# Loading the second query weight from ScalarE's DMA queue, beside the second K block

## The chip, the cores and the metric

The kernel runs on one NeuronCore of one Trainium2 chip. The metric is the device time of one execution in microseconds (us); lower is better.

## The reference

Two independent attention blocks, A and B, are computed for one new token each (decode), and their outputs are put side by side. Both have 32 heads of width 128 and a cache of 8192 keys and values in bf16; here B also has one K/V head per query head, so both blocks do the same work.

```python
def block(x, k_cache, v_cache, wq, wo):          # x [1,1,512], wq [512,4096], wo [4096,512]
    q = (x @ wq).reshape(1, 1, 32, 128).transpose(0, 2, 1, 3)
    scores = einsum("bhqd,bhkd->bhqk", q, k_cache) * 128 ** -0.5   # caches [1,32,8192,128]
    p = softmax(scores, axis=-1)
    o = einsum("bhqk,bhkd->bhqd", p, v_cache)
    return o.transpose(0, 2, 1, 3).reshape(1, 1, 4096) @ wo
out = concatenate([block(A...), block(B...)], axis=-1)             # [1,1,1024] bf16
```

Each cache element is used once, so the kernel mostly moves data: 4 caches of 67 MB, and 4 weights of 4 MB.

## The kernel before

The 64 heads are taken four at a time, in `NM` = 16 steps (0 to 7 belong to A, 8 to 15 to B). A step `n` loads one K block and one V block of four heads, 8192 KB each: a partition holds 256 rows of one head, in one run of 64 KB. K blocks go to the two slots of `kn`, V blocks to the single buffer `vn`. A query weight `wq` is 4096 KB, 32 KB per partition, and the two of them are put into the two halves of `vn` before the first V block needs that space.

In a step, VectorE (DVE) multiplies K in place by the broadcast query in four chunks (`plan_mul`, L348), TensorE (PE) adds up groups of products by matmuls with an identity (`plan_red`, L357), DVE finishes the sums (`plan_sr`, L368), finds the maxima (`plan_max`, `plan_gmax`, L374 and L383), ScalarE (ACT) takes the exponentials (L405), and one step later PE multiplies them with V (`plan_pv`, L426). All 128 partitions get the query from `plan_q`: for each half of a block's heads a group of 16 matmuls reads `wq` (L326) and ACT copies the result from PSUM to `qbc` (L334).

Every engine's program is an ordered list. `op` appends an instruction behind waits for what it `needs`; `dma` appends a transfer to the list of the engine that issues it. Before the change SyncE (SP) issues all loads, in the order in which the planner meets them:

- A's `wq` and the two rows `x`, K of step 0, B's `wq`;
- K of step 1, which waits for the copies of `x` (`x_ready`), because `x` lies in its slot;
- V of step 0, which waits for `q_done[1]`, the last query matmul of B, because both `wq` lie in `vn`;
- K of step 2, which waits for the last reduction of step 0 (`red_done`), then V of step 1 (waits for `pv_done` of step 0), K of step 3, and so on.

On PE, the two query groups of A come first. Those of B stand in step 0 behind the third reduction and ahead of the fourth. On ACT, the two copies of `x` and the two copies for A come first, then the two copies for B, then step 0's exponentials.

The order around the change, with the planner's calls:

```python
load_k(0)
load_wq(1)
plan_sel()
for j in range(QA // 4):
    plan_q(0, j)
for n in range(NM):
    ...
```

Of the kernel before, what the change touches and what calls it, by code (L numbers as in the profile page):

```python
# [11 lines left out]
P = 128  # L12
# [11 lines left out]
class _Plan:  # L24
# [15 lines left out]
    def op(self, eng, fn, ctr=None, needs=(), inc=1):  # L40

        for m in needs:
            self.wait(eng, m)
        self.prog[eng].append((fn, ctr, inc))
        if ctr is None:
            return None
        ctr.n += inc
        return ctr, ctr.n
# [81 lines left out]
def bass_concat_heads__mha_block_cached__gqa_block_cached__decode_kernel(  # L130
# [16 lines left out]
    wqs = [A_wq, B_wq]  # L147
# [27 lines left out]
    with ExitStack() as st:  # L175
# [8 lines left out]
        def flat(ap):  # L184
            return ap.rearrange("p t d -> p (t d)")
# [3 lines left out]
        wq_buf = [flat(vn[:])[:, a * W:(a + 1) * W] for a in range(NA)]  # L189
# [48 lines left out]
        def ctr(name):  # L238
            return _Ctr(nc, st, name)

        s_x = ctr("s_x")
        s_w = [ctr("s_w%d" % a) for a in range(NA)]
# [7 lines left out]
        def dma(eng, dst, src, c, needs=()):  # L250
            return op(eng, lambda e: e.dma_start(dst, src), c, needs, inc=16)  # L251
# [22 lines left out]
        k_in, v_in, wq_in, wo_in = {}, {}, {}, {}  # L274
# [6 lines left out]
        def load_k(n):  # L281
            k_in[n] = dma("SP", flat(kn[:, n % NK]), quad(ks, n), s_k[n % NK],
                          [x_ready if n == KX else red_done.get((n - NK, NCH - 1))])
# [4 lines left out]
                                [q_done[1] if n == 0 else pv_done[n - 1]]))  # L288
                       for i, (t0, t1) in enumerate(zip(cuts, cuts[1:]))]

        def load_wq(a):
            wq_in[a] = dma("SP", wq_buf[a], wqs[a].rearrange("(p c) n -> p (c n)", p=P), s_w[a])

        def load_wo(a, g):
            h0, n = WOG[a][g]
            src = wos[a][h0 * Dh:(h0 + n) * Dh, :].rearrange("(p j) n -> p (j n)", p=P)
            wo_in[a, g] = dma("SP", wo_sb[a][:, h0:h0 + n, :].rearrange("p j n -> p (j n)"), src,
                              s_wo[a][g], [red_done[NM - 2, NCH - 1]])


        load_wq(0)
        x_in = [dma("SP", xrow[0:1, a, :], xs[a][0], s_x) for a in range(NA)][-1]

# [14 lines left out]
        def plan_q(a, j):  # L318

            def mm(e):  # L320
                r = None
                for hh in range(G):
                    for c in range(C):
                        w = wq_sb[a][:, c, 4 * G * j * Dh:4 * G * (j + 1) * Dh].rearrange(
                            "p (i h d) -> p i h d", h=G, d=Dh)[:, :, hh, :]
                        r = e.matmul(  # L326
                            qyp[hh * HP:(hh + 1) * HP, :].rearrange("p (i d) -> p i d", d=Dh),
                            xb[:, a, c, hh * HP:(hh + 1) * HP], w,
                            start=(c == 0), stop=(c == C - 1))
                return r  # L330
            m = op("PE", mm, c_pe, [x_ready, wq_in[a], qy_free[0]])
            q_done[a] = m
            n0 = a * QA + 4 * j
            qy_free[0] = op("ACT", lambda e: e.copy(  # L334
                qbc[:, n0:n0 + 4, :].rearrange("p i d -> p (i d)"), qyp[:]), c_act, [m])
            for n in range(n0, n0 + 4):
                qbc_ready[n] = qy_free[0]
# [8 lines left out]
        def plan_mul(n, c):  # L346
            k = kn[:, n % NK, c * CT:(c + 1) * CT, :]
            mul_done[n, c] = op("DVE", lambda e: e.tensor_tensor(  # L348
                k, k, qbc[:, nth(n), :].broadcast_to([P, CT, Dh]), ALU.mult),
                c_mul, [k_in[n], qbc_ready[n]])  # L350

        def plan_red(n, c):

            def mm(e, i0):
                r = None
                for i in range(Dh // DW):
                    r = e.matmul(  # L357
                        rps[:, c % 2, :].rearrange("p (t d) -> p t d", d=DW), ident[:],
                        kn[:, i0, c * CT:(c + 1) * CT, i * DW:(i + 1) * DW],
                        start=(i == 0), stop=(i == Dh // DW - 1))  # L360
                return r
            by_slot = (n % NK, [lambda e, i=i: mm(e, i) for i in range(NK)])
            red_done[n, c] = op("PE", by_slot, c_red, [
                i_ident, mul_done[n, c],
                sr_done[n, c - 2] if c > 1 else sr_done.get((n - 1, c + NCH - 2))])

        def plan_sr(n, c):
            sr_done[n, c] = op("DVE", lambda e: e.tensor_reduce(  # L368
                s_sb[:, c * CT:(c + 1) * CT],
                rps[:, c % 2, :].rearrange("p (t d) -> p t d", d=DW), AX.X, ALU.add),  # L370
                c_sr, [red_done[n, c], p_done.get(n - 1)])

        def plan_max(n):
            m_done[n] = op("DVE", lambda e: e.tensor_reduce(  # L374
                m1[:], s_sb[:], AX.X, ALU.max), c_dve, [sr_done[n, NCH - 1]])
# [33 lines left out]
        def plan_sum(n):  # L409
            m = op("PE", lambda e: e.matmul(misc[:, 0:G], ones_f[:], rsum[:],  # L410
                                            start=True, stop=True), c_pe,
                   [p_done[n], misc_free[0]])
            r_done[n] = misc_free[0] = op("DVE", lambda e: e.reciprocal(
                rinv[:, nth(n), :].rearrange("p o g -> p (o g)"), misc[:, 0:G]), c_dve, [m])

        def plan_pv(n, t0, t1):
            for t, landed in v_in[n]:
                if t < t1:
                    wait("PE", landed)
            wait("PE", p_done[n])  # L420
            wait("PE", o_done.get(n - 1))

            def mm(e):
                r = None
                for t in range(t0, t1):
                    r = e.matmul(acc[:, 0:G], vn[:, t, :], pt[:, t, :],  # L426
                                 start=(t == 0), stop=(t == T - 1))
                return r
            if t1 == T:
                pv_done[n] = op("PE", mm, c_pv)  # L430
            else:
                op("PE", mm)

        def plan_o(n):
            o_done[n] = op("DVE", lambda e: e.tensor_tensor(  # L435
                oD[:].rearrange("p a h -> p (a h)")[:, nth(n, G)], acc[:, 0:G],
                rinv[:, nth(n), :].rearrange("p o g -> p (o g)"), ALU.mult),
                c_dve, [pv_done[n], r_done[n]])
# [4 lines left out]
        def plan_sel():  # L443
            sel_ready[0] = op("DVE", lambda e: e.tensor_reduce(
                sel[:, QR - 1:QR], ident[:, 0:P:QR], AX.X, ALU.max), c_dve, [i_sel0, i_ident])
            for g in RG:
                v = ident[:].rearrange("p (s j) -> p s j", j=g)
                op("DVE", lambda e, g=g, v=v: e.tensor_reduce(mask[g][:], v, AX.X, ALU.max),
                   c_dve, [i_ident])
                sel_ready[g] = op("DVE", lambda e, g=g, v=v: e.tensor_reduce(  # L450
                    jsel[g][:], v.rearrange("p s j -> p j s"), AX.X, ALU.max), c_dve)
# [108 lines left out]
        dcuts = []  # L560

        load_k(0)
        load_wq(1)
        plan_sel()
        for j in range(QA // 4):
            plan_q(0, j)
        for n in range(NM):
            if n >= L0:
                cuts[n].append(len(pl.prog["PE"]))
                dcuts.append(len(pl.prog["DVE"]))  # L570
            if n + 1 < NM:
                load_k(n + 1)
            else:
                load_wo(0, 0)
                for g in range(BEFORE):
                    load_wo(1, g)
            plan_mul(n, 0)
            plan_red(n, 0)
            plan_mul(n, 1)
            plan_red(n, 1)  # L580
            plan_sr(n, 0)
            plan_mul(n, 2)
            plan_red(n, 2)
            plan_sr(n, 1)
            plan_mul(n, 3)
            plan_sr(n, 2)
            if n == 0:
                for j in range(QA // 4):
                    plan_q(1, j)
            else:  # L590
                cuts[n].append(len(pl.prog["PE"]))
                plan_sum(n - 1)
                for t0, t1 in zip(VLAST, VLAST[1:]):
                    plan_pv(n - 1, t0, t1)
                cuts[n].append(len(pl.prog["PE"]))
                plan_o(n - 1)
            plan_red(n, 3)
            plan_sr(n, 3)
            plan_max(n)
            plan_gmax(n)  # L600
            plan_exp(n)
            load_v(n, VLAST if n == NM - 1 else (0, T))
# [119 lines left out]
```

## Time and profile before

| | |
|---|---|
| time, median of 3 runs | 666.3 us (666.25 to 666.35) |
| span of the profiled execution | 665.0 us |
| the profiled execution's own time | not given apart from its span; the median is 1.3 us above the span |
| PE busy | 440.2 us (66%) |
| DVE busy | 342.1 us (51%) |
| ACT busy | 62.4 us (9%) |
| bytes moved | 285.32 MB, mean 429 GB/s |

A profile is of one execution. Times in it are from its first instruction. Engine names with a q (SPq, ACTq) are the sequencers that issue transfers; a transfer's time to landing runs from its issue to the semaphore that says that all of it is there. In a timeline a row has the start, the duration, the engine, the line, the operation and how many were merged (x16); in brackets stands how long the engine had been idle and what released it. In the chain of waits a row has start, duration and what was waited for. Rows of queues give packets, MB and the share of the time of 16 DMA engines.

### The profile page before, as it was taken

The page shows a single profiled execution, that of the slowest core. Times are in us where ns is not written, and L with a number is a line of the kernel's source. Part 1 is how long each engine was busy: PE and PEld are TensorE (multiplying, and loading weights), DVE is VectorE, ACT ScalarE, POOL GpSimd, SP SyncE. Part 2 cuts the span into 40 slices and gives each one's busy share as a digit, 9 for nine tenths or more (in the row PEclk, how much of TensorE's full clock was granted, in tenths as well). Part 3 has the DMA queues.
Part 4 walks back from the last instruction along what each step waited for, and adds up shares of the span by engine and source line. Part 5 has one row for each costly group of instructions (what it writes and reads, how often), then busy time and mean ns, then how long its engine had stood idle before and what let it go on. Part 6 is the DMA issues. An engine that isn't in the chain of part 4 may idle for free.

```text
span 665.0 us, 12196 instructions
## 1 busy us (share of the span) xinstructions
PE 440.2 (66%) x5513; PEld 249.2 (37%) x5513; DVE 342.1 (51%) x218; ACT 62.4 (9%) x151; POOL 3.0 (0%) x15
## 2 busy tenths in 40 slices
PE   1166857848488594838759383875948387594875
PEld 0022343616135261614526161452616144262625
DVE  1085907466390746639073663908356380835620
ACT  1002002020200102020010202010020201002020
POOL 1000000000000000000000000000000000000000
PEclk9999857768786676878667687966768796676885
DMA  9999999999999999999999999999999999999997
GB/s 380 436 447 435 439 428 438 414 439 438 426 438 441 434 438 418 438 438 422 441 441 434 438 418 438 434 426 441 441 434 434 418 441 434 426 441 441 404 438 317
DMA packets 6069, 285.32 MB, mean 429 GB/s; under 512 B 683, under 2 KB 942, under 8 KB 1198
## 3 DMA queue, kind: packets, MB, share of 16 engines
q1 hardware_dynamic: 6056, 285.22, 99.3%
q8 instruction: 5, 0.08, 0.0%
q14 instruction: 2, 0.02, 0.0%
q10 hardware_dynamic: 6, 0.00, 0.0%
HBM read 285.21 MB, written 0.00 MB: 429 GB/s over the span
## 4 chain that ended last, share of the span: by engine, by line
DMA 65%; PE 24%; DVE 8%; issue 2%; SPq 0%; ACT 0%; DVEq 0%
DMA kn<-in_B_k_cache_dram 20%; DMA kn<-in_A_k_cache_dram 17%; DMA vn<-in_A_v_cache_dram 14%; PE rps L357 13%; PE acc L426 10%; DMA vn<-in_B_v_cache_dram 9%; DVE kn L348 8%; DMA kn<-in_B_wo_dram 4%; PE qyp L326 0%; SPq L251 0%; DVE s_sb L368 0%; PE yrow L538 0%; ACT qbc L334 0%; PE misc L410 0%; DVEq L348 0%
## 5 line engine op out<-in xcount | busy, mean ns | idle before, releaser
L357 PE MATMUL rps<-kn,ident 128*128 128x512 bf16 x1024 | 290.4, 451 | 168.4 <-DVE kn L348 165.3
L348 DVE TENSOR_TENSOR kn<-kn,qbc 128x8192 bf16<-128x8192 bf16 x64 | 281.5, 4419 | 93.3 <-DMA kn<-in_A_k_cache_dram 53.8
L357 PEld LDWEIGHTS rps<-kn,ident 128*128 128x128 bf16 x1024 | 111.4, 113 | 334.5 <-issue 258.1
L426 PE MATMUL acc<-pt,vn 128*128 128x4 bf16 x4096 | 109.3, 165 | 10.9 <-DMA vn<-in_B_v_cache_dram 5.9
L426 PEld LDWEIGHTS acc<-pt,vn 128*128 128x128 bf16 x4096 | 108.5, 101 | 11.8 <-DMA vn<-in_B_v_cache_dram 6.3
L368 DVE TENSOR_REDUCE s_sb<-rps 128x64 f32<-128x512 f32 x64 | 44.0, 688 | 110.9 <-PE rps L357 110.9
L405 ACT ACTIVATE pt<-s_sb,negb 32x256 bf16<-32x256 f32 x64 | 54.8, 857 | 1.9
L397 ACT ACTIVATE negb<-bmp 128x1 f32<-128x1 f32 x16 | 2.7, 171 | 526.6 <-PE bmp L393 526.6
L435 DVE TENSOR_TENSOR oD<-acc,rinv 128x4 f32 (+1 forms) x16 | 2.6, 162 | 96.3 <-PE acc L426 96.3
L393 PE MATMUL bmp<-gm,hrow 1*128 1x1 f32 x128 | 18.4, 260 | 6.0 <-DVE gm L383 6.0
L393 PEld LDWEIGHTS bmp<-gm,hrow 1*128 1x128 f32 x128 | 17.1, 203 | 10.7 <-DVE gm L383 10.0
L380 PE MATMUL mtp<-ident_f,m 128*1 128x128 f32 x32 | 6.1, 271 | 19.8 <-DVE m L374 19.8
L405 ACT ACTIVATION_READ_ACCUMULATOR pt<-s_sb,negb 32x1 f32 x64 | 15.9, 248 | 0.0
L380 PEld LDWEIGHTS mtp<-ident_f,m 128*1 128x1 f32 x32 | 1.4, 81 | 27.7 <-DVE m L374 27.7
L308 PE MATMUL misc<-ones_bf,kn 1*128 1x128 bf16 x4 | 0.6, 305 | 13.0 <-DMA kn<-in_B_x_dram 13.0
L383 DVE TENSOR_REDUCE gm<-mtp 1x4 f32<-1x128 f32 x16 | 4.5, 279 | 7.5 <-PE mtp L380 7.5
L326 PE MATMUL qyp<-vn,xb 128*32 128x512 bf16 x64 | 6.0, 505 | 2.2 <-ACT qbc L334 1.5
L410 PEld LDWEIGHTS misc<-rsum,ones_f 128*128 128x128 f32 x32 | 6.0, 190 | 2.9 <-issue 0.7
L374 DVE TENSOR_REDUCE m<-s_sb 128x1 f32<-128x256 f32 x16 | 6.7, 420 | 0.5
L334 ACT CAST qbc<-qyp 128x512 bf16<-128x512 f32 x4 | 2.3, 586 | 39.3 <-PE qyp L326 39.3
L308 PEld LDWEIGHTS misc<-ones_bf,kn 1*128 1x128 bf16 x4 | 0.3, 132 | 13.0 <-DMA kn<-in_B_x_dram 13.0
L410 PE MATMUL misc<-rsum,ones_f 128*128 128x4 f32 x32 | 4.6, 214 | 0.7 <-DVE oz L485 0.7
(53 smaller groups left out, 33.8 us busy)
## 6 DMA issues: line engine op xcount, KB each, us to landing
vn<-in_B_v_cache_dram SPq DMA_DIRECT2D x1, 6144.0 KB, 22.3
vn<-in_A_wq_dram SPq DMA_DIRECT2D x1, 4096.0 KB, 13.2
vn<-in_B_wq_dram SPq DMA_DIRECT2D x1, 4096.0 KB, 40.8
kn<-in_A_wo_dram SPq DMA_DIRECT2D x1, 4096.0 KB, 35.8
kn<-in_B_wo_dram SPq DMA_DIRECT2D x1, 2048.0 KB, 40.3
vn<-in_B_v_cache_dram SPq DMA_DIRECT2D x1, 2048.0 KB, 26.8
kn<-in_B_wo_dram SPq DMA_DIRECT2D x1, 1024.0 KB, 28.8
kn<-in_B_wo_dram SPq DMA_DIRECT2D x1, 512.0 KB, 29.6
```

The lines of the kernel that those rows point to most:

```text
L326: r = e.matmul(qyp[hh * HP:(hh + 1) * HP, :].rearrange("p (i d) -> p i d", d=Dh), xb[:, a, c, hh * HP:(hh + 1) * HP], w, start=(c == 0), s ...
L348: mul_done[n, c] = op("DVE", lambda e: e.tensor_tensor(k, k, qbc[:, nth(n), :].broadcast_to([P, CT, Dh]), ALU.mult), c_mul, [k_in[n], qbc_ ...
L357: r = e.matmul(rps[:, c % 2, :].rearrange("p (t d) -> p t d", d=DW), ident[:], kn[:, i0, c * CT:(c + 1) * CT, i * DW:(i + 1) * DW], start= ...
L368: sr_done[n, c] = op("DVE", lambda e: e.tensor_reduce(s_sb[:, c * CT:(c + 1) * CT], rps[:, c % 2, :].rearrange("p (t d) -> p t d", d=DW), ...
L374: m_done[n] = op("DVE", lambda e: e.tensor_reduce(m1[:], s_sb[:], AX.X, ALU.max), c_dve, [sr_done[n, NCH - 1]])
L380: m = op("PE", lambda e: e.matmul(mtp[0:1, 0:P], m1[:], ident_f[:], start=True, stop=True), c_pe, [m_done[n], i_identf, gm_done.get(n - 1)])
L383: gm_done[n] = op("DVE", lambda e: e.tensor_reduce(gm[:], mtp[0:1, 0:P].rearrange("o (h p) -> o h p", h=G), AX.X, ALU.max), c_dve, [m, nb_ ...
L393: r = e.matmul(bmp[:, 0:1], hrow[0:1, (G - 1 - h) * HP:(G - 1 - h) * HP + P], gm[0:1, h:h + 1], start=(h == 0), stop=(h == G - 1))
L397: nb_done[n] = op("ACT", lambda e: e.activation(negb[:, n:n + 1], bmp[:, 0:1], AF.Copy, scale=-scale), c_act, [m])
L405: p_done[n] = op("ACT", lambda e, h=h, q=q: e.activation(pt[q, :, h], s_sb[q, :], AF.Exp, bias=negb[q, n:n + 1], scale=scale, accum_out=rs ...
L410: m = op("PE", lambda e: e.matmul(misc[:, 0:G], ones_f[:], rsum[:], start=True, stop=True), c_pe, [p_done[n], misc_free[0]])
L426: r = e.matmul(acc[:, 0:G], vn[:, t, :], pt[:, t, :], start=(t == 0), stop=(t == T - 1))
```

## The change

`load_wq` takes the issuing engine and its waits as arguments. B's `wq` is no longer issued by SP between K of step 0 and K of step 1. It is issued by ACT, behind A's two query copies in ACT's list, and ACT first waits for K of step 0 to land (`k_in[0]`). SP issues K of step 1 as before, when `x` has been copied, and so it is next on SP's queue behind K of step 0. Buffers, sizes and the waits of all users stay as they were.

```diff
-        def load_wq(a):
-            wq_in[a] = dma("SP", wq_buf[a], wqs[a].rearrange("(p c) n -> p (c n)", p=P), s_w[a])
+        def load_wq(a, eng="SP", needs=()):
+            wq_in[a] = dma(eng, wq_buf[a], wqs[a].rearrange("(p c) n -> p (c n)", p=P), s_w[a],
+                           needs)
...
         load_k(0)
-        load_wq(1)
         plan_sel()
         for j in range(QA // 4):
             plan_q(0, j)
+        load_wq(1, "ACT", [k_in[0]])
         for n in range(NM):
```

## Prediction

> **What bounds the kernel now.** I read the page's span, slices and queues first, then the DMA view cut to the middle of the run.
>
> ```profile
> span 665.0 us, 12196 instructions
> DMA  9999999999999999999999999999999999999997
> q1 hardware_dynamic: 6056, 285.22, 99.3%
> q10 hardware_dynamic: 6, 0.00, 0.0%
> ...
> DMA packets 5618, 284.46 MB, mean 432 GB/s; under 512 B 619, under 2 KB 622, under 8 KB 755
> q1 hardware_dynamic: 5609, 284.36, 100.0%
> ```
>
> The last two lines are of the window 2 to 660 us. All bytes run on queue q1, which SyncE (SP) feeds; q10 is ScalarE's (ACT's), with only the three output stores. In 658 us q1 fills all 16 DMA engines to 100.0%: the kernel is a stream of 285 MB at 432 GB/s with a short head and tail. Two things follow. Reordering the same bytes can win almost nothing. And a stretch in which the DMA engines have nothing to do is added to the end one for one, however much TensorE (PE) or VectorE (DVE) idles.
>
> The median is 666.3 us and the span 665.0, so 1.3 us lie around it. I work in differences and add them to the median.
>
> Next the issue times, from the timeline of SP's queue, and two landings from the list of DMA issues.
>
> ```profile
> 0.80 0.38 SPq L251 DMA_DIRECT2D vn<-in_A_wq_dram  x1
> 1.88 0.36 SPq L251 DMA_DIRECT2D kn<-in_A_k_cache_dram  x1
> 2.28 0.53 SPq L251 DMA_DIRECT2D vn<-in_B_wq_dram  x1
> 14.75 0.33 SPq L251 DMA_DIRECT2D kn<-in_A_k_cache_dram  x1
> 55.82 0.33 SPq L251 DMA_DIRECT2D vn<-in_A_v_cache_dram  x1
> 59.33 0.33 SPq L251 DMA_DIRECT2D kn<-in_A_k_cache_dram  x1
> 92.75 0.33 SPq L251 DMA_DIRECT2D vn<-in_A_v_cache_dram  x1
> 102.23 0.33 SPq L251 DMA_DIRECT2D kn<-in_A_k_cache_dram  x1
> 129.35 0.33 SPq L251 DMA_DIRECT2D vn<-in_A_v_cache_dram  x1
> ...
> vn<-in_A_wq_dram SPq DMA_DIRECT2D x1, 4096.0 KB, 13.2
> vn<-in_B_wq_dram SPq DMA_DIRECT2D x1, 4096.0 KB, 40.8
> ```
>
> Call the loads wqA, K0, wqB, K1, V0, K2, V1, K3, V2 in this order. wqB lands at 2.28 + 40.8 = 43.1 us. K0, K1 and V0 are seen in the chain of waits and on DVE:
>
> ```profile
> 1.88 31.47 DMA kn<-in_A_k_cache_dram
> 33.37 4.44 DVE kn L348
> 55.82 26.22 DMA vn<-in_A_v_cache_dram
> 82.09 4.03 PE acc L426 x150
> 62.85 8.76 DVE L348 TENSOR_TENSOR kn<-kn,qbc 128x8192 bf16<-128x8192 bf16 x2 [1.62 <-DMA kn<-in_A_k_cache_dram]
> ```
>
> K0 lands at 33.35, K1 at 62.85, V0 at 82.04. So wqB took 43.1 - 33.35 = 9.7 us of the stream, V0 82.04 - 62.85 = 19.2 us, and wqB and K1 together 62.85 - 33.35 = 29.5 us. V0 was issued at 55.82, 7 us before the queue ran dry of K1. That lead is what the change spends from: V0 may not be issued before the two query matmul groups of B (L326) have read wqB, because it overwrites the same buffer.
>
> **What is removed, added and moved.** Removed: SP's issue of wqB at 2.28 (0.53 us). SP then waits for the x copies until 14.75 in any case; worth nothing. Added: a wait of ACT for K0 and one DMA issue on ACT. Its engine rows around that time:
>
> ```profile
> 19.47 0.59 ACT L334 CAST qbc<-qyp 128x512 bf16<-128x512 f32 x1 [2.08 <-PE qyp L326]
> 54.02 0.59 ACT L334 CAST qbc<-qyp 128x512 bf16<-128x512 f32 x1 [33.96 <-PE qyp L326]
> ```
>
> ACT is idle from 20.1 to 54.0 and K0 lands at 33.35, so wait and issue lie inside that idle time: nothing queued behind them is late. If that cover were gone, the cost would be the issue itself, up to 0.5 us.
>
> Moved: wqB leaves its place between K0 and K1. K1 now follows K0 directly, and wqB competes with K1 from about 34.4 us (33.4 plus some 1.0 us to start, from the output stores below). The bytes are the same, so both are in at about 62.85 as before. The whole question is which ends last: wqB had 43.1, and PE asks for it at 52.84.
>
> ```profile
> 14.78 1.93 PE L326 MATMUL qyp<-vn,xb 128*32 128x512 bf16 x16 [0.74 <-ACT xb L312]
> 17.45 1.93 PE L326 MATMUL qyp<-vn,xb 128*32 128x512 bf16 x16 [0.73 <-ACT qbc L334]
> 37.94 9.68 PE L357 MATMUL rps<-kn,ident 128*128 128x512 bf16 x32 [18.57 <-DVE kn L348]
> 49.28 3.63 PE L357 MATMUL rps<-kn,ident 128*128 128x512 bf16 x16 [1.66 <-DVE kn L348]
> 52.84 1.08 PE L326 MATMUL qyp<-vn,xb 128*32 128x512 bf16 x16
> 54.66 1.08 PE L326 MATMUL qyp<-vn,xb 128*32 128x512 bf16 x16 [0.74 <-ACT qbc L334]
> 55.67 3.63 PE L357 MATMUL rps<-kn,ident 128*128 128x512 bf16 x16
> ```
>
> How two filled queues share an engine, the trace of before barely shows: q10 has just one transfer beside a full q1, the store of out_row (1 KB) near the end. Its issue, then the DMA view from 646.7 to 650.9, then from 650.9 to 651.0, then the last store and SP's wait for it:
>
> ```profile
> 646.69 0.51 ACTq L251 DMA_DIRECT2D out_dram<-out_row  x1
> ...
> DMA packets 42, 1.90 MB, mean 453 GB/s; under 512 B 2, under 2 KB 2, under 8 KB 2
> q1 hardware_dynamic: 42, 1.90, 104.7%
> ...
> q10 hardware_dynamic: 2, 0.00, 3.8%
> ...
> 663.74 0.27 SPq L251 DMA_DIRECT2D out_dram<-out_q  x1
> SPq L693 <- DMA out_dram<-out_q: 1.0, 1, 1.0
> ```
>
> On idle queues a store is through in about 1.0 us. Beside the full q1, the 1 KB of out_row moved only after 4.2 us, while q1's packets of about 1.90 MB / 40 = 47 KB went ahead: that is one partition's run of the load then in flight. So a packet, not a few bytes, looks like the unit in which an engine changes queues, and a newcomer waits for one or two of them. K1 has 64 KB per partition and wqB 32 KB, each 8 runs per engine (128 partitions over 16 engines). Taking turns run by run, wqB gets a third of the rate and its eighth run comes after K1's eighth. If engines take turns by whole transfers instead, K1 goes first and wqB again ends last. Either way wqB lands at about 62.85 instead of 43.1. I take that as the likeliest.
>
> The Trainium skill, "DMA: Bandwidth & Descriptors", section "Queues, rings and completion order", says that each DMA engine goes round the queues that have work and drains a whole packet of one before it switches. The 4.2 us agree, and by that rule shares equal in bytes are not to be had; it lowers the chance that I give them below.
>
> Then PE waits from 52.9 to 62.85, and the two query groups follow. After long idle time PE is slow: the groups at 14.78 took 1.93 us against 1.08 later, and at 37.94, after 18.57 us of idle time, 32 matmuls took 9.68 against twice 3.63. With 10 us of idle time I take the slow price: 14.78 to 17.45 + 1.93 = 19.38, 4.6 us, and 0.1 to SP's issue. The fast price is 55.82 - 52.84 = 3.0 us, 1.7 less. V0 is issued at 62.85 + 4.7 = 67.5.
>
> The Trainium skill, "TensorE: Matmul & The Clock Gate", Part 1, puts the clock at half after an idle window of about 3.4 us. The trace agrees as far as 1.93 against 1.08 goes; by that rule the chain is 4.7 us, without it 3.0.
>
> V0 now meets an empty queue. Its landing lies between 67.5 + 1.0 + 19.2 = 87.7 (start as for the last store) and 67.5 + 13.2 + 9.7 = 90.4 (as for wqA, which also met an empty queue, and 4096 KB more), against 82.04: 5.7 to 8.4 us later. Neither row is nearer, so I take the middle, **7.1 us**. With the fast price of the query groups the lower end is 4.0.
>
> Does this shift pass to the end, or grow? K1's last reduction now starts at about 67.6 instead of 55.67 and ends by 67.6 + 6.2 (the cold price of 16 matmuls, below) = 73.8 instead of 59.33; DVE reaches K1's multiply 1.9 us later as before, so by 75.7 rather than 62.85: iteration 1 is up to 12.8 us late. V1's issue moves from 92.75 to at most 105.6. The stream has V0 until 89.1 and K2 until 108.3, so V1 comes with some 2 us in hand. K3 (102.23 + 12.8 = 115.0) goes behind V1, V2 (129.35 + 12.8 = 142.2) comes before V1 and K3 end at 146.7. No second gap, but the margin is small.
>
> ```profile
> 37.94 6.24 PE rps L357 x16
> 60.95 0.28 DVE L383 TENSOR_REDUCE gm<-mtp 1x4 f32<-1x128 f32 x1 [0.47 <-PE mtp L380]
> ```
>
> (The 1.9 us run from 59.33 to 60.95 + 0.28 = 61.23, where DVE is through with K0's maximum and free for K1.) From there on the stream is full again, and its lead is never regained: 666.3 + 7.1 = **673.4 us**.
>
> **Rivals.** *Equal shares, no change.* If an engine splits its rate evenly by bytes, wqB takes twice 9.7 us from 34.4 to 37.6 (the newcomer's 4.2 us) on: it lands at 53.8 to 57.0, V0 is issued 3.0 us later, at 56.8 to 60.0, and still finds K1 in flight until 62.85 with over the 1.0 us that a start needs. The stream has no gap: 666.3, give or take 0.5. It decides if wqB lands before about 58.8. For it: q1's own stream gives no sign of how shares fall between two big transfers. Against it: the 4.2 us of out_row. A start of wqB so late that the change does not do what it says (no overlap with K1 at all) ends as the forecast does, since wqB then lands last.
>
> *Sharing costs rate.* If the engines lose time at every change of queue, the mixed stretch is longer than 29.5 us. The lowest slice on the page bounds it:
>
> ```profile
> GB/s 380 436 447 435 439 428 438 414 439 438 426 438 441 434 438 418 438 438 422 441 441 434 438 418 438 434 426 441 441 434 434 418 441 434 426 441 441 404 438 317
> ```
>
> 380 GB/s in the first slice, which has the start-up in it: wqB and K1 are 12.58 MB, 33.1 us at that rate, 3.6 us more. Added to the forecast this gives 677.0. For it: two read streams have never run side by side here. Against it: the stream beside out_row kept 453 GB/s.
>
> *Faster.* Nothing on the page is shortened; closing the small seams between loads in one 29.5 us stretch is worth under 0.5 us.
>
> **The numbers.** Forecast (wqB last, one gap) 0.68, its own range 666.3 + 4.0 = 670.3 to 666.3 + 8.4 = 674.7; sharing that costs rate on top 0.10; equal shares 0.19; faster by over 0.2% 0.03. A difference of about 0.2% (1.3 us) is what a measurement can tell from none. A little of equal shares, with wqB landing just too late, ends slower: faster 0.03, same 0.18, slower 0.79. The two cases that end slower hold under 0.8 between them, so the range reaches to equal shares, 665.8, and up to both upper bounds, 666.3 + 8.4 + 3.6 = 678.3.
>
> **What would show it.** Right: wqB issued by ACT at about 33.4 and landing about 29 us later; PE waiting from 52.9 to about 62.9 for wqB with the groups at L326 at 1.93 us each; V0 issued near 67.5; DMA busy share falling for some 5 us before 70; V0's landing near 89; all later issues some 7 us later at an unchanged 432 GB/s. Wrong: wqB landing before 58, V0's issue before 61 and no dip (no change); or a second dip near 105 (a larger loss); or a low rate from 34 to 63.

## The result, and the profile after

| | median | range | ratio to before |
|---|---|---|---|
| before | 666.33 us | 666.25 to 666.37 | |
| changed | 674.92 us | 674.60 to 674.99 | 1.0127 (1.0115 to 1.0140) |

The change costs 8.6 us. The profiled execution took 674.99 us, with a span of 673.7.

From the page of the changed kernel: the span, the DMA slices and rates, and the queues.

```profile
span 673.7 us, 12196 instructions
DMA  9995999999999999999999999999999999999997
GB/s 375 436 436 250 425 429 425 428 433 428 432 432 436 432 436 436 436 436 424 436 436 432 436 436 436 436 436 436 436 436 436 432 432 436 428 428 428 414 446 308
q1 hardware_dynamic: 5912, 281.02, 96.7%
q10 hardware_dynamic: 150, 4.20, 1.4%
```

One slice of 40 has fallen, the fourth (50.5 to 67.4 us): 250 GB/s. Everything behind it is as full as before, and q10 now carries wqB's 4.2 MB.

The timeline of the changed kernel around that slice, and two landings (K1 is issued within the pair that starts at 1.89):

```profile
1.89 13.33 SPq L251 DMA_DIRECT2D kn<-in_A_k_cache_dram  x2
67.63 0.33 SPq L251 DMA_DIRECT2D vn<-in_A_v_cache_dram  x1
103.59 0.33 SPq L251 DMA_DIRECT2D vn<-in_A_v_cache_dram  x1
...
32.96 0.38 ACTq L251 DMA_DIRECT2D vn<-in_B_wq_dram  x1
...
48.90 3.63 PE L358 MATMUL rps<-kn,ident 128*128 128x512 bf16 x16 [1.66 <-DVE kn L349]
62.95 1.93 PE L327 MATMUL qyp<-vn,xb 128*32 128x512 bf16 x16 [10.43 <-DMA vn<-in_B_wq_dram]
65.61 1.93 PE L327 MATMUL qyp<-vn,xb 128*32 128x512 bf16 x16 [0.73 <-ACT qbc L335]
...
vn<-in_B_wq_dram ACTq DMA_DIRECT2D x1, 4096.0 KB, 30.0
vn<-in_A_v_cache_dram SPq DMA_DIRECT2D x1, 23.1
```

wqB is issued as soon as K0 is in, and lands 30.0 us later, at 62.9 instead of 43.1. PE waits 10.43 us for it and runs the two query groups at 1.93 us each. V0 goes out at 67.63 and lands at 90.7; before, it landed at 82.0.

How K1 and wqB shared the engines is in the DMA view of the changed kernel from 38 to 58 us:

```profile
DMA packets 171, 8.37 MB, mean 419 GB/s; under 512 B 0, under 2 KB 0, under 8 KB 0
q1 hardware_dynamic: 85, 5.57, 64.3%
q10 hardware_dynamic: 85, 2.79, 32.4%
q8 instruction: 1, 0.02, 0.3%
```

85 packets against 85, twice the bytes on q1. The packets' starts and lengths in the trace show the turns: where a run of K1 (64 KB, 2.42 us) ends, a run of wqB (32 KB, 1.21 us) begins, and the other way round, with few exceptions. wqB got a third of the rate.

Where the 8.6 us lie is told by the windows of the changed kernel (the last two columns are the DMA share and GB/s; a packet counts whole in the window in which it starts):

```profile
33.40:60.00 26.60, 13.33 (x48) 5.14 (x48) 18.88 (x7) 0.00 (x0) 0.00 (x0) 0.94 0.99 429
60.00:62.90 2.90, 0.00 (x0) 0.00 (x0) 0.00 (x0) 0.00 (x0) 0.00 (x0) 0.50 0.11 45
62.90:68.50 5.60, 4.82 (x35) 1.54 (x36) 0.00 (x0) 1.17 (x2) 0.00 (x0) 0.50 0.00 0
68.50:71.50 3.00, 3.00 (x12) 1.18 (x10) 0.00 (x0) 0.00 (x0) 0.00 (x0) 0.71 1.05 371
```

Up to 60 us the mixed stretch loses nothing: share 0.99, 429 GB/s. The 0.11 behind it is of packets that start there, and those under way run on. By the packets' starts and lengths, the engines finish wqB's last run between 60.5 and 62.5 us, eleven of the sixteen by 60.9: on average 1.9 us before wqB lands at 62.9. From there to V0's issue at 67.63 nothing moves: 4.7 us. V0's first packets start 1.0 to 1.9 us after the issue, 1.3 on average, and take 3.0 us on average against 2.42 in the full stream: 0.6 more. Together 8.5 us, the difference but for 0.1.

The same packets show that it all lies there. Up to 60.5 us the changed kernel has moved as many bytes as the kernel before; from 27 MB to 280 MB it is 8.5 to 8.6 us late throughout.

### The profile page after: what moved, and what is told of

It is laid out like the page before. It is cut to its first block, busy times and chain, and to the rows that moved or that the text cites. A ratio compares the mean times of both kernels' runs of the same rounds, so it can differ in the third digit from the quotient of the medians.

```text
span 673.7 us, 12196 instructions
## 1 busy us (share of the span) xinstructions
PE 446.1 (66%) x5513; PEld 249.7 (37%) x5513; DVE 342.1 (51%) x218; ACT 62.5 (9%) x151; POOL 3.0 (0%) x15
## 4 chain that ended last, share of the span: by engine, by line
DMA 60%; PE 27%; DVE 10%; issue 2%; SPq 0%; ACT 0%; DVEq 0%
DMA kn<-in_B_k_cache_dram 20%; DMA kn<-in_A_k_cache_dram 17%; PE rps L358 16%; PE acc L427 10%; DMA vn<-in_A_v_cache_dram 9%; DVE kn L349 9%; DMA vn<-in_B_v_cache_dram 5%; DMA vn<-in_B_wq_dram 4%; DMA kn<-in_B_wo_dram 4%; PE qyp L327 1%; DVE s_sb L369 0%; SPq L251 0%; PE yrow L539 0%; DVE m L375 0%; PE misc L411 0%
## 5 line engine op out<-in xcount | busy, mean ns | idle before, releaser
L358 PE MATMUL rps<-kn,ident 128*128 128x512 bf16 x1024 | 295.6, 457 | 163.0 <-DVE kn L349 159.3
L327 PE MATMUL qyp<-vn,xb 128*32 128x512 bf16 x64 | 7.7, 627 | 12.6 <-DMA vn<-in_B_wq_dram 10.4
L327 PEld LDWEIGHTS qyp<-vn,xb 128*32 128x32 bf16 x64 | 2.2, 128 | 17.1 <-DMA vn<-in_B_wq_dram 10.9
```

What stands on the lines that cost most here:

```text
L327: r = e.matmul(qyp[hh * HP:(hh + 1) * HP, :].rearrange("p (i d) -> p i d", d=Dh), xb[:, a, c, hh * HP:(hh + 1) * HP], w, start=(c == 0), s ...
L358: r = e.matmul(rps[:, c % 2, :].rearrange("p (t d) -> p t d", d=DW), ident[:], kn[:, i0, c * CT:(c + 1) * CT, i * DW:(i + 1) * DW], start= ...
```

## Experiments

Labels K0, wqB, V0 and so on are those of the prediction. Each kernel was timed against the kernel before on the same chip (666.4 to 666.5 us there).

**wqB behind K1 on SP's queue.** Is it the second queue, or the order?

```diff
 (before)
         load_k(0)
-        load_wq(1)
...
                 load_k(n + 1)
+                if n == 0:
+                    load_wq(1)
```

> wqB stays on SP's queue and is issued right behind K1; ACT issues no load and q10 carries none. Theory (the loss comes from wqB landing last, whichever queue carries it): wqB lands at about 62.9 us, V0 is issued near 67.6 on an empty queue, and the time is that of the changed kernel, 674.9 give or take 0.7. Rival (the loss comes from running two queues side by side, or from ACT's issue and wait): 666.3.

Measured: 674.89 us, ratio 1.0126 (1.0110 to 1.0143). Its SP and PE rows and wqB's landing:

```profile
15.19 0.43 SPq L251 DMA_DIRECT2D vn<-in_B_wq_dram  x1
67.35 0.33 SPq L251 DMA_DIRECT2D vn<-in_A_v_cache_dram  x1
...
62.67 1.93 PE L326 MATMUL qyp<-vn,xb 128*32 128x512 bf16 x16 [10.23 <-DMA vn<-in_B_wq_dram]
...
vn<-in_B_wq_dram SPq DMA_DIRECT2D x1, 4096.0 KB, 47.4
```

The same loss with one queue and no work for ACT: what costs is that wqB lands last, at 62.6, not who issues it. The rival of a second queue's cost is out.

**ACT issues wqB without the wait for K0.**

```diff
-        load_wq(1, "ACT", [k_in[0]])
+        load_wq(1, "ACT")
```

> wqB is issued by ACT, but without the wait for K0, so at about 20 us, beside K0. Theory (the engines take turns run by run, 64 KB of K against 32 KB of wqB, and only the time of wqB's landing matters): wqB's eight runs are through at about 53 us; K0 lands 4 to 5 us later (37 to 38), PE reaches B's queries at about 57, V0 is issued at about 60 while K1 still runs: 666.3 to 667.5. Rival (a load on ACT's queue costs rate or a start): stays near 675. Rival (turns by whole transfers): wqB lands right after K0, V0 is issued at about 56: 666.3.

Measured: 668.21 us (667.21 to 669.06), ratio 1.0024 (1.0014 to 1.0034), above the 667.5 that was allowed.

```profile
19.39 0.38 ACTq L251 DMA_DIRECT2D vn<-in_B_wq_dram  x1
...
39.37 4.43 DVE L349 TENSOR_TENSOR kn<-kn,qbc 128x8192 bf16<-128x8192 bf16 x1 [33.54 <-DMA kn<-in_A_k_cache_dram]
...
61.63 0.33 SPq L251 DMA_DIRECT2D vn<-in_A_v_cache_dram  x1
...
vn<-in_B_wq_dram ACTq DMA_DIRECT2D x1, 4096.0 KB, 32.6
```

wqB lands at 52.0, as turns run by run had it (53). The price has moved to K0, which lands at 39.4 instead of 33.4 (37 to 38 expected), and so PE's queue of work is late: V0 goes out at 61.63, with K1 nearly through. Most of the loss is gone, with the load still on ACT's queue; that V0 comes later than 60 leaves 1.7 us in the median, and 2.6 in the profiled execution, which is the slowest of the ten (669.06).

**K blocks in two halves, changed and before.** With runs of 32 KB on both sides, wqB should have half of the rate.

```diff
-            k_in[n] = dma("SP", flat(kn[:, n % NK]), quad(ks, n), s_k[n % NK], [...])
+            dst, src, half = flat(kn[:, n % NK]), quad(ks, n), T * Dh // 2
+            for u in range(2):
+                k_in[n] = dma("SP", dst[:, u * half:(u + 1) * half],
+                              src[:, u * half:(u + 1) * half], s_k[n % NK], [...])
```

> The changed kernel with every K block loaded by two transfers of 32 KB per partition instead of one of 64 KB. Theory (turns run by run): K1's and wqB's runs are now of one size, wqB gets half of the rate and lands at about 56 us; V0 is issued by 61 with K1 still in flight, so the loss is gone: within 1.5 us of the same kernel with wqB back on SP (e4). Rival (cost of a second queue, or wqB last in any case): 8 us above e4.

> Control: the kernel before with every K block loaded in two halves. Each 64 KB run becomes two of 32 KB. Both theories: 666.3 to 668.

Measured: 671.11 us changed (ratio 1.0069, 1.0052 to 1.0086), 667.58 before (1.0018, 1.0008 to 1.0027): 3.5 us apart, neither the 1.5 of the theory nor the 8 of the rival. The changed one's rows, and its queues from 38 to 57 us:

```profile
33.22 0.38 ACTq L251 DMA_DIRECT2D vn<-in_B_wq_dram  x1
...
58.09 1.93 PE L330 MATMUL qyp<-vn,xb 128*32 128x512 bf16 x16 [6.60 <-DMA vn<-in_B_wq_dram]
62.77 0.33 SPq L251 DMA_DIRECT2D vn<-in_A_v_cache_dram  x1
...
q1 hardware_dynamic: 146, 4.26, 52.0%
q10 hardware_dynamic: 128, 3.70, 45.3%
```

The sharing is as expected: nearly equal bytes, and wqB lands 5 us earlier, at 58.0. But that is 2 us later than I had it, PE has idled 6.60 us and takes the slow 1.93 us per group, and V0 leaves at 62.77. So the expectation missed the size: equal shares would not have hidden the load.

**PE kept busy while it waits.** 40 matmuls whose result nobody reads stand ahead of B's query groups; they are added work.

```diff
             if n == 0:
+                def fill(e):
+                    r = None
+                    for _ in range(40):
+                        r = e.matmul(misc[:], zero[:],
+                                     ident[:, None, :].broadcast_to([P, NQ, P]), start=True, stop=True)
+                    return r
+                op("PE", fill, c_pe, [i_zero, i_ident, x_ready])
                 for j in range(QA // 4):
                     plan_q(1, j)
```

> The changed kernel with 40 extra matmuls (zeros times the identity, 128x512, read by nobody) on PE ahead of B's queries, to keep PE busy while it waits for wqB. Theory (the two query groups and the copy between them are slow because PE stood idle, and lie on the path): the groups take 1.08 us instead of 1.93 and V0 is issued 1.6 us earlier: 673.2. Rival (idle time is not why they are slow, or they are not on the path): 674.9.

Measured: 673.66 us (673.12 to 674.18), ratio 1.0111 (1.0094 to 1.0127).

```profile
62.60 1.08 PE L327 MATMUL qyp<-vn,xb 128*32 128x512 bf16 x16 [1.69 <-DMA vn<-in_B_wq_dram]
65.58 0.33 SPq L251 DMA_DIRECT2D vn<-in_A_v_cache_dram  x1
```

The groups take 1.08 us; the granted clock from 62.60 to 65.60 was 1.00, against 0.50 in the changed kernel's windows above. V0 leaves 2.05 us earlier (0.35 of it because wqB landed earlier), and the profiled execution is 1.9 us faster than that of the changed kernel (673.12 against 674.99). The median fell by 1.3 of the 1.7 expected, and two of the four times are near each end of the range: the term is on the path, its size in the median is only roughly shown.

**V0 in two halves.** The first half of V0 overwrites A's wq only and waits for A's queries; the second waits for B's.

```diff
-                                [q_done[1] if n == 0 else pv_done[n - 1]]))
+                                [q_done[i] if n == 0 else pv_done[n - 1]]))
...
-            load_v(n, VLAST if n == NM - 1 else (0, T))
+            load_v(n, VLAST if n == NM - 1 else (0, T // 2, T) if n == 0 else (0, T))
```

(Both halves of V0 count on the first semaphore.)

> The changed kernel with V0 loaded in two halves: the first goes into the space of A's wq and waits only for A's queries, so it is on the queue behind K1 long before wqB lands; the second waits for B's queries as before. Theory with one gap only: V0's first half covers the 67.6 us at which its second half is issued, the loss is gone: 666.3. Theory with a second wait behind it: step 0's last reduction still stands behind B's queries on PE, so V1 is issued at about 103.6 as in the changed kernel, while the stream, now without the first gap, runs dry at about 101; V1 lands at 103.6 + 23.1 = 126.7 against 120.7: 672.4.

Measured: 674.18 us (672.15 to 674.81), ratio 1.0119 (1.0102 to 1.0136); the profiled execution is the one at 672.15. Its SP rows, and the DMA view from 101 to 105:

```profile
73.73 0.33 SPq L251 DMA_DIRECT2D kn<-in_A_k_cache_dram  x1
103.75 0.33 SPq L251 DMA_DIRECT2D vn<-in_A_v_cache_dram  x1
...
DMA packets 16, 0.67 MB, mean 168 GB/s; under 512 B 5, under 2 KB 5, under 8 KB 5
```

The first gap has shrunk, and a second one stands behind it: V1 leaves at 103.75 and the stream is dry before. By the bytes moved, this execution is 1.0 us late once V0's second half has started, and 5.7 us once V1 has. wqB, which now shares with V0's first half too, lands later, at 65.1. B's query groups on PE hold back step 0's last reduction, and that makes step 1 late as well. The one-gap theory (666.3) falls; the 672.4 of the other is met by the profiled execution, while the median is 1.8 us above. What the other executions had beyond the profiled one's 5.7 us is not shown.

**B's query groups behind step 0's last reduction on PE**, alone and with V0 in halves.

```diff
-            if n == 0:
-                for j in range(QA // 4):
-                    plan_q(1, j)
-            else:
+            if n > 0:
                 cuts[n].append(len(pl.prog["PE"]))
...
             plan_exp(n)
+            if n == 0:
+                for j in range(QA // 4):
+                    plan_q(1, j)
```

> The changed kernel with only B's query groups moved on PE behind step 0's last reduction; V0 in one transfer. Theory: V0 still waits for wqB, 674.9 less at most 1.7 (PE idles for less time before the groups); step 0's lateness alone costs nothing in the changed kernel. Rival (PE's late reductions make the loss): well under 672.

> As e5, and B's query groups moved on PE behind step 0's last reduction and its exponentials' broadcast. Theory with a second wait: both covers together leave no gap: V1 is issued by 96, 666.3 to 667. Theory with one gap only: the same as e5.

Measured: alone 674.79 us, ratio 1.0125 (1.0108 to 1.0142); with V0 in halves 667.89 us (666.48 to 668.42), ratio 1.0018 (1.0009 to 1.0028). SP's rows with both:

```profile
19.45 50.62 SPq L251 DMA_DIRECT2D vn<-in_A_v_cache_dram  x2
93.48 0.33 SPq L251 DMA_DIRECT2D vn<-in_A_v_cache_dram  x1
```

In the changed kernel the late reduction costs nothing, since the first gap has already moved the stream behind it. With the first gap nearly covered it is what is late next; with both changes, V1 leaves at 93.48 and 7.0 of the 8.6 us are back although wqB lands later still, at 65.1. The profiled execution (668.42) is 2.0 us above before. By the bytes moved, 1.0 of them is lost between V0's halves: the issue of the second ends at 70.07, when the engines begin to run out of the first. The rest shows only at the end of the run and is open; the kernel's own times spread over 1.9 us. Nothing here beats the kernel before, whose stream had no gap to close.

## Why the prediction was right

The mechanism went as the prediction laid it down, up to the end.

- *What bounds.* A full stream, where a gap is added one for one: right. V0's landing is 8.7 us late (90.7 against 82.0) and the total 8.6. (q10 had two of the three output stores, not all three; SP issued the other. Nothing rests on it.)
- *ACT's wait and issue, SP's missing issue.* Worth nothing, as said: without either, wqB last on SP's queue gives 674.89.
- *wqB lands at 62.85.* 62.9. The turns run by run, inferred from one 1 KB store, are now shown directly by 85 packets against 85 and by their order. The Trainium skill, "DMA: Bandwidth & Descriptors", "Queues, rings and completion order", has a turn as a packet, typically of 9 to 17 descriptors; here a turn was one run of 64 or 32 KB, so that transfers share by the lengths of their runs.
- *The slow query groups, 4.7 us.* Right: 62.95 to 67.63, with 1.93 us each, and 1.08 where PE had been kept busy.
- *The restart, 5.7 to 8.4 us in all, taken as 7.1.* This term was mis-sized, by 1.5 us; the measured total lies just above the likeliest case's own upper end (674.7). It is inside the whole range only because that one reaches up by the 3.6 us of the rate rival, which did not come about: so much of it is luck. I counted the gap from 62.85, wqB's landing, and that is when the last of 16 engines is through. The 19.2 us of the lower bound run from landing to landing in a full stream: in the kernel before, the engines began V0 between 60.4 and 62.3 us, ahead of K1's landing at 62.85. On an empty queue this head start is missing, 1.9 us, and the first packets were 0.6 us slower; neither is in the lower bound. By the same count V0's lead before was 4.6 us to the first engine that was through with K1, not 7. The row of wqA, which gave the upper end (22.9 us from issue to landing, measured 23.1), was the nearer one, and the middle was no reasoned choice.
- *No second gap.* Right for the changed kernel (V1 issued at 103.59, at most 105.6 forecast; no second slice down). The reduction that the prediction calls K1's there is step 0's, which reads K0; it took 4.96 us, not 6.2. That the margin was thin is confirmed by V0 in halves, where the same lateness makes a gap.
- *Rivals.* Shares that cost rate: wrong, the same bytes as before had moved by 60.5 us. Equal shares, no change: it did not come about, and its price was wrong too. With nearly equal bytes the loss was 3.5 us; I had given it the fast query groups and a deadline at K1's landing, both too kind.

The V0 issues and losses, put side by side, show the true deadline (K halves against their own control). V0's issue is seen in the profiled execution alone, so the loss of that execution stands beside it, its time less the median before:

| kernel | wqB lands | V0 issued | its loss | median loss |
|---|---|---|---|---|
| before | 43.1 | 55.8 | 0 | 0 |
| ACT without the wait | 52.0 | 61.63 | 2.6 | 1.7 |
| changed, K in halves | 58.0 | 62.77 | 3.6 | 3.5 |
| changed, PE kept busy | 62.5 | 65.58 | 6.7 | 7.2 |
| wqB behind K1 on SP | 62.6 | 67.35 | 8.5 | 8.4 |
| changed, B's queries last on PE | 62.8 | 67.55 | 8.4 | 8.4 |
| changed | 62.9 | 67.63 | 8.7 | 8.6 |

In all six rows below the first, the issue less its loss is 58.9 to 59.2 us: one for one, the loss would end at an issue of about 59.0. No run issued V0 in one transfer between 55.8 and 61.6, so this is read off the line. V0 has to leave about 4 us before the last load ahead of it lands (62.9), not 1.0 us; the engines run dry from 60.5 on, and V0's packets start 1.0 to 1.9 us after the issue.

## What to carry to other kernels

In a kernel that streams without a gap, look at what a moved load releases, not only at when its own user needs it: here a small weight that lands 20 us later holds the buffer of the next large load. A transfer that was put on a second queue was not served sooner here, nor in equal shares; it shared by the length of its runs, and counting turns gave its landing to within 2 us (53 for 52.0, 56 for 58.0). Count a dry queue from the first engine that runs out, not from the landing of the last (60.5 and 62.9 us here); and when one gap is covered, check which issue is late next.

## What the hardware showed unexpectedly

Two loads on two queues ran side by side at full rate: 429 GB/s up to 60 us, with a change of queue at nearly every packet. An empty stream is dear to start again: 23.1 us from issue to landing for a block that takes 19.2 us in the full stream, with first packets that start 1.0 to 1.9 us after the issue and take 3.0 us on average against 2.42. A transfer's landing is that of its last engine: for wqB the sixteen ended 2.0 us apart.
